# A planner's transfer price, its waits between engines and its table of shifts replaced

## The chip, the cores and the metric

The kernel runs on one core of a Trainium2 chip. The metric is the time of one execution on the device in microseconds (us). Engines are named as the profile names them: PE (TensorE), DVE (VectorE), ACT (ScalarE), POOL (GpSimd) and SP (SyncE, whose queue issues the transfers).

## The reference

Three stages follow one another. The output of one is the input of the next, and all inputs but q, k and v are weights.

```
# 1 attention: B=4, H=8, S=1152, D=64; queries averaged in pairs, so 576 rows
q_pool = q.reshape(B, H, S // 2, 2, D).mean(axis=3)
scores = (1 / np.sqrt(D)) * np.matmul(q_pool, k.transpose(0, 1, 3, 2))
scores = scores - np.max(scores, axis=-1, keepdims=True)
attn = np.exp(scores)
attn = attn / (np.sum(attn, axis=-1, keepdims=True) + 1e-09)
x = heads_side_by_side(np.matmul(attn, v))            # (4, 576, 512)
# 2 token mixing over the 576 rows, then a channel part
h = np.maximum(xt @ w_tok1, 0.0) @ w_tok2             # xt = x transposed; 576 -> 256 -> 576
u = x + h.transpose(0, 2, 1)
x = u + np.maximum(u @ w_ch1, 0.0) @ w_ch2            # 512 -> 1536 -> 512
# 3 Fourier mixing, a norm over the channels, a channel part
u = x + np.real(np.fft.fft(np.fft.fft(x, axis=1), axis=2))
un = (u - mean(u)) / np.sqrt(var(u) + 1e-06)
out = u + np.maximum(un @ w_ch1, 0.0) @ w_ch2         # 512 -> 2048 -> 512
```

The weights arrive as 64-bit floats.

## The kernel before, in words

Every fp32 operand of a product is split into a high and a low part of a shorter format, and a product is the sum of several matmuls of such parts. Attention works in 32 units, one for each batch and head: scores and their row maxima (line 655 on PE, line 662 on DVE, the exponential in line 665 on ACT), transposes of the exponentials (line 808), their split (line 812 on ACT, 815 on DVE) and the product with v (line 822). Some units at the start use another form (lines 758 to 773). Beside attention run the token mixing and the channel part of stage 2 for batches whose heads are done (lines 913 to 1051). Then come the Fourier mixing as matmuls with tables (line 1168), the norm and the transposes of line 1290, and the first channel rows of stage 3 (lines 1309 to 1347). The last stage is lines 1425 to 1514: products of line 1455 go into one of three PSUM banks, ACT copies them out (1465), DVE adds (1469), and line 1514 multiplies the result by the second weight.

A 64-bit weight is converted on the chip, in 62 pieces of up to 512 KB. Each piece has a buffer "slot" of a ring. SP loads it (line 375); ACT takes the absolute value of the high words (377) and turns the low words into floats (390); POOL clamps (379), DVE shifts, signs and masks (381, 384, 387), POOL multiplies and adds (392, 394), ACT takes the high part (397), POOL the low part (399), and SP stores the result to memory (410, 413), from where later steps load it again.

Nothing waits for a clock: each engine runs its own instructions in the order in which they are recorded, and stands still where the first of them waits, whatever is behind it. All transfers are issued by SP. The order is made before that by a planner, class Plan. Every step is added with a key, an engine, a cost in us, a due time, the steps that it depends on and the buffers that it takes or reads. SHIFT moves the due time of all steps of one key. The method "order" then replays the program: at each moment every free engine takes, of its ready steps, that with the earliest due time whose buffers are free. A step's end is the moment plus its cost; "lag" says how long after that a step on another engine may start, and "free_lag" when its buffers count as free. For a transfer, with t_dma as its cost, the replay reads

```
free["DMA"] = max(free.get("DMA", 0.0), now + 1.3) + best.cost
best.end, busy = free["DMA"] + 0.7, now + 0.35
```

so a transfer that finds no other ahead of it counts as landed 1.3 us, its cost and 0.7 us after its issue. The costs decide the order and nothing else.

## Time and profile before

| | us |
|---|---|
| median of three runs | 1481.97 |
| fastest, slowest run | 1467.82, 1483.97 |
| the profiled execution | 1484.98 |
| its span | 1482.9 |
| busy: PE, DVE, ACT, POOL | 1405.7, 981.3, 754.8, 573.9 |
| mean granted clock of TensorE | 0.976 of full speed |

The span is the time from the first to the last instruction that the profiler saw. In a timeline row the columns are start, duration, engine, line, operation, output and inputs, shapes and count; a bracket at the end tells how long the engine was idle before it and whose result ended that idle time. In a group row they are line, engine, operation, shapes and count, then busy time in all and the mean in ns, then idle time before the group and what ended it.

### The profile page before, as it was taken

How to read it: one execution, taken by the hardware profiler on the slowest of the kernel's cores; microseconds unless marked ns; L12 is line 12 of the kernel's file. 1: busy time of each engine (PE TensorE's matmuls, PEld its weight loads, DVE VectorE, ACT ScalarE, POOL GpSimd, SP SyncE). 2: the span in 40 equal slices, each digit the busy share in tenths (PEclk: the TensorE clock that was granted, in tenths of full speed). 3: DMA queues.
4: the chain of work that ended last, by engine and by line, in shares of the span. 5: the costliest groups of instructions: out<-in, count | busy, mean ns of one | idle time of the engine just before them, and what ended most of it. 6: DMA issues, size and time to landing. Idle time of an engine off the chain costs nothing.

```text
span 1482.9 us, 24363 instructions
## 1 busy us (share of the span) xinstructions
PE 1405.7 (95%) x9019; PEld 1281.9 (86%) x9019; DVE 981.3 (66%) x1830; ACT 754.8 (51%) x1534; POOL 573.9 (39%) x471
## 2 busy tenths in 40 slices
PE   7999989999999998998999999999899999999998
PEld 5777768899988898998999998999889888888887
DVE  6676547788876877887787776666555755465432
ACT  4444557866656766666785554422234443253230
POOL 4567766767668786685672001021010000000000
PEclk7999989999999999999999999999999999999999
DMA  7667658677758786776775216765074644544532
GB/s 176 181 191 194 175 182 247 211 209 245 229 148 270 182 258 203 219 216 201 235 207 161 86 57 180 262 199 163 17 232 151 217 160 157 181 159 153 174 110 93
DMA packets 112176, 270.34 MB, mean 182 GB/s; under 512 B 9971, under 2 KB 37748, under 8 KB 111767
## 3 DMA queue, kind: packets, MB, share of 16 engines
q1 hardware_dynamic: 112058, 268.79, 59.8%
q8 instruction: 71, 1.16, 0.3%
q14 instruction: 47, 0.39, 0.1%
HBM read 191.15 MB, written 44.86 MB: 159 GB/s over the span
## 4 chain that ended last, share of the span: by engine, by line
PE 63%; DMA 14%; DVE 7%; issue 6%; ACT 5%; POOL 3%; SPq 2%; ACTq 0%; DVEq 0%; POOLq 0%
PE bank L1455 8%; PE bank L1012 7%; PE y L1514 7%; PE bank L992 6%; PE m L655 5%; PE av L822 4%; PE av L769 4%; PE c L1514 4%; DMA slot<-in_wm_dram 4%; PE s L758 2%; PE bank L1325 2%; PE y L1347 2%; PE bank L689 2%; PE bank L808 2%; DVE nm L662 2%
## 5 line engine op out<-in xcount | busy, mean ns | idle before, releaser
L662 DVE TENSOR_REDUCE nm<-m 128x1 f32<-128x1152 f32 (+1 forms) x120 | 162.1, 1351 | 42.9 <-PE m L655 42.1
L992 PE MATMUL bank<-ut,w 128*128 128x320 f32 (+1 forms) x1152 | 178.4, 298 | 3.1 <-DVE yt L1021 2.0
L655 PE MATMUL m<-kk,qq 128*128 128x384 f32 (+1 forms) x720 | 157.8, 351 | 15.4 <-ACT s L665 15.2
L1455 PE MATMUL bank<-tt,wc 128*128 128x320 f32 x1008 | 161.5, 313 | 6.8 <-ACT e L1465 4.9
L665 ACT ACTIVATE s<-m,nm 128x1152 f32<-128x1152 f32 (+1 forms) x120 | 146.5, 1221 | 41.1 <-DVE nm L662 40.2
L1455 PEld LDWEIGHTS bank<-tt,wc 128*128 128x128 f32 x1008 | 149.4, 188 | 20.4 <-ACT e L1465 9.4
L1012 PE MATMUL bank<-h,w 128*128 128x320 f32 (+1 forms) x1152 | 164.3, 298 | 2.6 <-DVE yt L1021 1.3
L992 PEld LDWEIGHTS bank<-ut,w 128*128 128x128 f32 x1152 | 161.1, 190 | 4.4 <-DVE yt L1021 2.3
L1012 PEld LDWEIGHTS bank<-h,w 128*128 128x128 f32 x1152 | 156.6, 189 | 5.4 <-DVE pl L815 2.6
L655 PEld LDWEIGHTS m<-kk,qq 128*128 128x128 f32 (+1 forms) x720 | 119.8, 183 | 24.6 <-ACT s L665 19.7
L379 POOL TENSOR_SCALAR slot<-slot 128x512 f32<-128x512 f32 (+2 forms) x62 | 119.1, 1925 | 51.1 <-ACT slot L377 47.6
L822 PE MATMUL av<-ph,vv 128*128 128x256 f32 (+1 forms) x432 | 128.6, 317 | 0.5 <-DVE xtr L834 0.4
L812 ACT ACTIVATE ph<-bank 128x512 fp32r<-128x512 f32 (+1 forms) x192 | 90.1, 471 | 68.7 <-PE bank L808 67.0
L822 PE MATMUL av<-pl,vv 128*128 128x256 f32 (+1 forms) x432 | 119.7, 297 | 0.5 <-DVE pl L815 0.3
L815 DVE TENSOR_TENSOR pl<-bank,ph 128x512 fp32r<-128x512 f32 (+1 forms) x192 | 100.2, 523 | 23.2 <-ACT ph L812 22.2
L392 POOL TENSOR_TENSOR slot<-slot 128x512 f32<-128x512 f32 (+2 forms) x62 | 82.5, 1335 | 82.5 <-DVE slot L387 76.7
L1021 DVE TENSOR_TENSOR yt<-bank,yt 128x256 f32<-128x256 f32 (+1 forms) x192 | 85.7, 452 | 35.0 <-PE bank L1012 33.5
L1514 PE MATMUL y<-v,hp 128*128 128x512 f32 x432 | 104.8, 391 | 0.0
L1476 DVE SCALAR_TENSOR_TENSOR hp<-e,hp 128x320 fp32r<-128x320 f32 x96 | 41.7, 486 | 92.2 <-ACT hp L1474 91.9
L1474 ACT ACTIVATE hp<-e 128x320 fp32r<-128x320 f32 x96 | 38.3, 461 | 124.4 <-PE y L1514 116.8
L815 DVE TENSOR_TENSOR pl<-tr,ph 128x512 fp32r<-128x512 f32 (+1 forms) x144 | 79.2, 550 | 24.5 <-ACT ph L812 23.9
L808 PE MATMUL bank<-ident,s 128*128 128x128 f32 (+1 forms) x600 | 92.8, 270 | 0.7 <-DVE pl L815 0.6
(162 smaller groups left out, 2950.5 us busy)
## 6 DMA issues: line engine op xcount, KB each, us to landing
w<-wb_d SPq DMA_DIRECT2D x96, 512.0 KB
slot<-in_wm_dram SPq DMA_DIRECT2D x56, 512.0 KB
v<-w_d SPq DMA_DIRECT2D x24, 1024.0 KB
raw<-w_d SPq DMA_DIRECT2D x24, 896.0 KB
kk<-kx SPq DMA_DIRECT2D x66, 288.0 KB
wb_d<-slot SPq DMA_DIRECT2D x24, 512.0 KB
v<-in_v_dram SPq DMA_DIRECT2D x32, 292.5 KB
kx<-in_kT_dram SPq DMA_DIRECT2D x15, 576.0 KB
```

The costliest lines, as they stand in the source:

```text
L379: a = add("cclamp", "P", 0.155 + n * 0.00347, due, lambda: nc.gpsimd.tensor_scalar(out=f32(hi()), in0=f32(hi()), scalar1=F64_LO, scalar2=F ...
L655: nc.tensor.matmul(m.t[:n, :KW], qq.t[:r, t, q0:q0 + n], kk.t[:r, c * KW:(c + 1) * KW], start=(t == 0), stop=(t == 1))
L662: a = add("mx" + own_place, "V", t_dve(S), d + 0.05, lambda n=n, j=j: nc.vector.tensor_reduce(out=nm.t[:n, j:j + 1], in_=m_tile[0][:n, :, ...
L665: o = add("exp" + own_place, "A", t_act(S) + 0.18, d + 0.1, lambda s=s, n=n, j=j: nc.scalar.activation(out=s.t[:n].rearrange("p (c n) -> p ...
L808: nc.tensor.transpose(ps.t[:, at:at + r], made[j][0].t[:r, c * 128:(c + 1) * 128], ident[:r, :r])
L812: a = add("hi", "A", t_act(n), due + 0.1, lambda ps=ps, ph=ph, n=n: nc.scalar.activation(out=ph.t[:, :n], in_=ps.t[:, :n], func=AF.Copy), ...
L815: b = add("lo", "V", t_dve(n), due + 0.2, lambda ps=ps, ph=ph, pl=pl, n=n: nc.vector.tensor_tensor(out=pl.t[:, :n], in0=ps.t[:, :n], in1=f ...
L822: nc.tensor.matmul(po.t[:, :nq], vv.t[:, c].rearrange("p s d -> p (s d)"), x.t[:, k * nq:(k + 1) * nq], start=c == 0 and x is ph, stop=c = ...
L992: mms.append(lambda ps, k=len(mms), kk=kk, wi=wi, xi=xi, t0=t0, n=n: nc.tensor.matmul(ps[:, :n], view("p (s k n) -> p s k n", s=2, k=4)[:, ...
L1012: mms.append(lambda ps, k=len(mms), x=x, wi=wi, hi=hi, cc=cc, t0=t0, n=n: nc.tensor.matmul(ps[:, :n], ww[x][2]("p (s n) -> p s n", s=2)[:, ...
L1455: nc.tensor.matmul(ps.t[:, :PH], w.t[:, wi, k, 128 * kk:128 * kk + 128], x.t[:, xi, kk], start=(first and m == 0), stop=(last and m == 5), ...
L1514: nc.tensor.matmul(y.t, h.t[:, k, hi, j * 128:(j + 1) * 128], v.t[:, wi, k], start=(q == 0 and k == 0 and n == 0), stop=(q == 7 and k == 1 ...
```

## The change

The table SHIFT has new values for all its keys. A transfer costs its bytes over 235e3 instead of 390e3 per us, and the factors 1.2 and 1.75 on the loads and copies of q and k are gone. An engine is free only at the full end of a step, where the old account let the next step on ACT, DVE or POOL start 0.04 to 0.1 us earlier; every hop from one engine to another costs 0.2 us (0.26 to PE), a step on DVE that follows one on DVE 0.13 us, and buffers are free 0.2 us after a step's end. The lines of the changed kernel are those of the kernel before less 11. The computation, its steps and their tiles are the same.

```diff
@@ -60,26 +60,26 @@
 SHIFT = {
-    "cvld": -31.09, "cabs": 1541.59, "cclamp": 706.11, "cshift": 873.83, "csign": 145.68, "cexp": 661.87,
...
+    "cvld": -25.93, "cabs": 1270.21, "cclamp": 705.49, "cshift": 902.44, "csign": -44.94, "cexp": 832.42,
...
@@ -117,7 +117,7 @@
         self.key = key
         self.moves = eng in ("SP", "AQ")
         eng = "A" if eng == "AQ" else eng
-        self.eng, self.cost, self.due, self.emit, self.new, self.uses = eng, max(cost, 0.16) if eng == "V" else cost, due, emit, new, uses
+        self.eng, self.cost, self.due, self.emit, self.new, self.uses = eng, cost, due, emit, new, uses
         self.deps, self.after = deps, after
         self.end = None
         self.next = []
@@ -129,21 +129,10 @@
 SHARED = ("TL", "TA", "LL", "WL", "cshift", "csign", "cexp", "FPUT", "dwl", "yadd", "ql.", "kl.", "q.", "un")
 
 
-OVERLAP = {"A": 0.1, "V": 0.083, "P": 0.04}
-
-
 def lag(a, b):
-    if b == "T":
-        return 0.0 if a == "T" else 0.16 if a in OVERLAP else 0.26
-    if a == "T" or a not in OVERLAP or b not in OVERLAP:
-        return 0.2
-    if a == b == "A":
-        return -0.1
-    return 0.08 if b == "P" else 0.035
-
-
-def free_lag(a):
-    return 0.13 if a in OVERLAP else 0.2
+    if a == b:
+        return 0.13 if a == "V" else 0.0
+    return 0.26 if b == "T" else 0.2
 
 
 class Plan:
@@ -204,7 +193,7 @@
                     free["lock"] = best.end
                 elif eng == "P":
                     best.end += max(0.0, free.get("lock", 0.0) - now)
-                busy = best.end - OVERLAP.get(eng, 0.0)
+                busy = best.end
                 if best.moves:
                     free["DMA"] = max(free.get("DMA", 0.0), now + 1.3) + best.cost
                     best.end, busy = free["DMA"] + 0.7, now + 0.35
@@ -212,7 +201,7 @@
                         busy = max(busy, free["DMA"] - 1.5)
                 free[eng] = busy
                 heapq.heappush(wait, (busy, -1))
-                heapq.heappush(wait, (best.end + (0.2 if best.moves else free_lag(eng)), -1))
+                heapq.heappush(wait, (best.end + 0.2, -1))
                 out.append(best)
                 for o in best.next:
                     o.left -= 1
@@ -222,7 +211,7 @@
         return out
 
     def done(self, b, now):
-        return all(u.end is not None and u.end + (0.2 if u.moves else free_lag(u.eng)) <= now for u in b.users)
+        return all(u.end is not None and u.end + 0.2 <= now for u in b.users)
 
     def over(self, ring, now):
         for k, b in enumerate(ring.live if ring.any_slot else ring.live[:1]):
@@ -330,7 +319,7 @@
             return n * 0.00221 + 0.155
 
         def t_dma(n):
-            return n / 390e3
+            return n / 235e3
 
         def mm(*a, **k):
             return partial(nc.tensor.matmul, *a, **k)
@@ -598,9 +587,9 @@
             b, h = divmod(2 * p, H)
             kx, qx = Buf(kx_r), Buf(qx_r)
             due = 4 * p - 4.5
-            lq = add("lq", "SP", 1.2 * t_dma(128 * 8 * NQ), due, lambda: nc.sync.dma_start(
+            lq = add("lq", "SP", t_dma(128 * 8 * NQ), due, lambda: nc.sync.dma_start(
                 out=f32(qx.t), in_=qT[b, h:h + 2].rearrange("h d t n -> (h d) t n")), new=[qx])
-            lk = add("lk", "SP", 1.2 * t_dma(128 * 4 * S), due, lambda: nc.sync.dma_start(
+            lk = add("lk", "SP", t_dma(128 * 4 * S), due, lambda: nc.sync.dma_start(
                 out=f32(kx.t)[:, 1], in_=kT[b, h:h + 2].rearrange("h d n -> (h d) n")), new=[kx])
             q = add("qs", "P", t_pool(NQ), due + 0.5, lambda: nc.gpsimd.tensor_tensor(
                 out=f32(qx.t)[:, 1], in0=f32(qx.t)[:, 0], in1=f32(qx.t)[:, 1], op=ALU.add), [lq], uses=[qx])
@@ -618,18 +607,18 @@
                 kk, qq = Buf(kk_r), Buf(qq_r)
                 r = slice(64 * (g % 2), 64 * (g % 2) + 64)
                 d = 2 * g - 2.8
-                loads = [add("stk", "SP", 1.75 * t_dma(64 * 4 * S), d, lambda kk=kk, r=r: nc.sync.dma_start(
+                loads = [add("stk", "SP", t_dma(64 * 4 * S), d, lambda kk=kk, r=r: nc.sync.dma_start(
                     out=f32(kk.t)[:64], in_=f32(kx.t)[r, 0]), [kh], new=[kk], uses=[kx])]
-                loads.append(add("stq", "SP", 1.75 * t_dma(64 * 8 * NQ), d, lambda qq=qq, r=r: nc.sync.dma_start(
+                loads.append(add("stq", "SP", t_dma(64 * 8 * NQ), d, lambda qq=qq, r=r: nc.sync.dma_start(
                     out=f32(qq.t)[:64, :, :NQ], in_=f32(qx.t)[r]), [ql, qh], loads[:1], new=[qq], uses=[qx]))
-                loads.append(add("stk", "SP", 1.75 * t_dma(64 * 4 * S), d, lambda kk=kk, r=r: nc.sync.dma_start(
+                loads.append(add("stk", "SP", t_dma(64 * 4 * S), d, lambda kk=kk, r=r: nc.sync.dma_start(
                     out=f32(kk.t)[64:], in_=f32(kx.t)[r, 1]), [kl], loads[:1], uses=[kx, kk]))
-                loads.append(add("stq", "SP", 1.75 * t_dma(64 * 4 * NQ), d, lambda qq=qq, r=r: nc.sync.dma_start(
+                loads.append(add("stq", "SP", t_dma(64 * 4 * NQ), d, lambda qq=qq, r=r: nc.sync.dma_start(
                     out=f32(qq.t)[64:, 0, :NQ], in_=f32(qx.t)[r, 0]), [qh], loads[1:2], uses=[qx, qq]))
                 k2 = z = None
                 if g < ALONE:
                     k2 = Buf(k2_r)
-                    loads.append(add("stk", "SP", 1.75 * t_dma(64 * 4 * S), d, lambda k2=k2, r=r: nc.sync.dma_start(
+                    loads.append(add("stk", "SP", t_dma(64 * 4 * S), d, lambda k2=k2, r=r: nc.sync.dma_start(
                         out=f32(k2.t)[:64], in_=f32(kx.t)[r, 0]), [kh], loads[:1], new=[k2], uses=[kx]))
                 if g < ALONE + 3:
                     z = add("qz", "P", 0.4, 2 * g - 2.5, lambda qq=qq: nc.gpsimd.memset(f32(qq.t)[64:66, 1], 0.0), loads[1:2], uses=[qq])
```

On ACT, in the middle of attention: the place of the conversion step of line 390 (379 in the changed kernel) that stands at 557 us in the trace before, and the corresponding conversion in the new order. "slot" is the conversion's buffer, "s" the scores, "ph" a high part. Before:

```order
L812 ACTIVATE ph<-bank 128x320
L812 ACTIVATE ph<-tr 128x320
L812 ACTIVATE ph<-bank 128x320
L665 ACTIVATE s,sum_157<-m,nm 128x1152
L913 ACTIVATE h<-bank 128x256
L812 ACTIVATE ph<-tr 128x320
L812 ACTIVATE ph<-bank 128x320
L812 ACTIVATE ph<-tr 128x320
L390 ACTIVATE slot<-slot 128x512
L665 ACTIVATE s,sum_157<-m,nm 128x1152
L812 ACTIVATE ph<-bank 128x320
L377 ACTIVATE slot<-slot 128x512
```

and in the changed kernel:

```order
L801 ACTIVATE ph<-tr 128x512
L772 ACTIVATE vv<-v 128x9x64
L598 ACTIVATE qx<-qx 128x576
L654 ACTIVATE s,sum_157<-m,nm 128x1152
L858 ACTIVATE x_5744<-xs 128x5x64
L379 ACTIVATE slot<-slot 128x512
L366 ACTIVATE slot<-slot 128x512
L379 ACTIVATE slot<-slot 128x512
L801 ACTIVATE ph<-bank 128x256
L366 ACTIVATE slot<-slot 128x512
L654 ACTIVATE s,sum_157<-m,nm 66x1152
L902 ACTIVATE h<-bank 128x256
```

The exponential of line 665 stands right behind the conversion step before; in the new order three conversion steps stand together ahead of a split of line 801, and the last exponential of the unit comes three places after them.

On PE, in the last stage: runs of products of line 1455 (1444) among those of line 1514 (1503). Before:

```order
L1455 MATMUL bank<-tt,wc 128x320 x36
L1514 MATMUL y<-v_15294,hp 128x512 x3
L1455 MATMUL bank<-tt,wc 128x320 x6
L1514 MATMUL y<-v_15294,hp 128x512 x15
L1514 MATMUL c<-v_15397,hp 128x512 x9
L1455 MATMUL bank<-tt,wc 128x320 x36
L1514 MATMUL c<-v_15397,hp 128x512 x3
L1455 MATMUL bank<-tt,wc 128x320 x6
L1514 MATMUL y<-v_15397,hp 128x512 x18
L1514 MATMUL c<-v_15500,hp 128x512 x12
```

and in the changed kernel:

```order
L1503 MATMUL c<-v_15163,hp 128x512 x9
L1444 MATMUL bank<-tt,wc 128x320 x42
L1503 MATMUL c<-v_15163,hp 128x512 x3
L1503 MATMUL y<-v_15163,hp 128x512 x18
L1503 MATMUL c<-v_15282,hp 128x512 x9
L1444 MATMUL bank<-tt,wc 128x320 x42
L1503 MATMUL c<-v_15282,hp 128x512 x3
L1503 MATMUL y<-v_15282,hp 128x512 x18
L1503 MATMUL c<-v_15386,hp 128x512 x12
L1503 MATMUL y<-v_15386,hp 128x512 x18
```

Before, six products of the seven of a block stand together, three matmuls of another product follow, and then the seventh; now all seven stand together.

On ACT, the end of the conversions, where the steps of line 390 (379) are the last of the program. Before:

```order
L812 ACTIVATE ph<-bank 128x512
L812 ACTIVATE ph<-tr 128x512
L783 ACTIVATE vv<-v 128x9x64
L390 ACTIVATE slot<-slot 128x512
L377 ACTIVATE slot<-slot 128x512
L812 ACTIVATE ph<-bank 128x256
```

and in the changed kernel:

```order
L858 ACTIVATE x_8833<-xs 128x5x64
L379 ACTIVATE slot<-slot 128x512
L366 ACTIVATE slot<-slot 128x512
L1578 ACT_TABLE_LOAD
L1578 ACTIVATE rooted<-eps 128x1
L1588 ACTIVATE ny<-wraw 1x258
L902 ACTIVATE h<-bank 128x256
L1093 ACTIVATE cs<-wraw 97x870
L902 ACTIVATE h<-bank 128x320
L379 ACTIVATE slot<-slot 128x512
L386 ACTIVATE slot<-slot 128x512
L366 ACTIVATE slot<-slot 128x512
```

Before, the last conversion starts among the splits of attention and is the last for good; in the new order the last two stand among the first tables of the Fourier mixing (lines 1578 to 1588 and 1093).

## Rows read from the trace of the kernel before

**Rows 1.** The page, part 1: busy us, share, instructions by engine.

```profile
PE 1405.7 (95%) x9019; PEld 1281.9 (86%) x9019; DVE 981.3 (66%) x1830; ACT 754.8 (51%) x1534; POOL 573.9 (39%) x471
```

**Rows 2.** Stretches: us, busy PE, PEld, DVE, ACT, POOL, granted clock, DMA share, GB/s.

```profile
205.00:887.00 682.00, 650.34 (x4708) 622.28 (x4708) 532.78 (x933) 449.45 (x931) 412.64 (x325) 0.98 0.66 197
...
760.00:887.00 127.00, 126.20 (x950) 123.16 (x949) 93.25 (x166) 73.31 (x153) 25.77 (x20) 1.00 0.37 116
...
1105.00:1482.90 377.90, 366.37 (x1980) 322.17 (x1980) 193.04 (x333) 137.07 (x256) 0.00 (x0) 1.00 0.47 157
```

**Rows 3.** Timeline of PE: gaps of over 1.3 us, late ACT results.

```profile
27.65 0.61 PE L758 MATMUL s<-qq,kk 128*128 128x288 f32 x1 [1.83 <-ACT s L763]
67.01 0.82 PE L758 MATMUL s<-qq,kk 128*128 128x288 f32 x4 [2.19 <-ACT s L763]
104.67 0.92 PE L758 MATMUL s<-qq,kk 128*128 128x288 f32 x4 [3.10 <-ACT s L763]
133.93 1.36 PE L758 MATMUL s<-qq,kk 128*128 128x288 f32 x6 [1.31 <-ACT s L763]
196.71 0.54 PE L758 MATMUL s<-qq,kk 128*128 128x288 f32 x2 [2.85 <-ACT s L763]
478.73 0.66 PE L808 MATMUL tr<-ident,s 128*128 128x128 f32 x4 [1.69 <-DVE pl L815]
559.01 1.21 PE L655 MATMUL m<-kk,qq 128*128 128x384 f32 x3 [2.67 <-ACT s L665]
588.41 1.33 PE L655 MATMUL m<-kk,qq 128*128 128x384 f32 x6 [2.23 <-ACT s L665]
679.90 0.50 PE L808 MATMUL tr<-ident,s 128*128 128x128 f32 x3 [1.90 <-DVE pl L815]
701.96 1.60 PE L927 MATMUL bank<-x,w 128*128 128x512 f32 x4 [2.06 <-ACT yo L1051]
```

**Rows 4.** Timeline of ACT ahead of two of these gaps.

```profile
557.11 0.65 ACT L390 ACTIVATE slot<-slot 128x512 f32<-128x512 uint32 x1 [2.85 <-DMA slot<-in_wm_dram]
...
678.34 0.67 ACT L390 ACTIVATE slot<-slot 128x512 f32<-128x512 uint32 x1 [3.51 <-DMA slot<-in_wm_dram]
```

**Rows 5.** Groups by line, ACT, whole span.

```profile
L390 ACT ACTIVATE slot<-slot 128x512 f32<-128x512 uint32 (+2 forms) x62 | 41.3, 668 | 61.3 <-DMA slot<-in_wm_dram 33.3 <-DMA slot<-in_wt_dram 11.5 <-issue 7.3
```

**Rows 6.** Chain of waits that ended last: start, us, the 512 KB loads.

```profile
550.05 6.95 DMA slot<-in_wm_dram
...
672.60 5.63 DMA slot<-in_wm_dram
```

**Rows 7.** Stretches at the lower clock, columns as in rows 2.

```profile
67.70:71.10 3.40, 2.98 (x9) 1.96 (x9) 1.96 (x2) 2.47 (x7) 3.40 (x3) 0.51 0.77 180
...
702.50:705.90 3.40, 3.40 (x10) 2.69 (x9) 0.61 (x3) 1.83 (x4) 3.40 (x8) 0.50 0.99 192
...
432.90:439.70 6.80, 5.96 (x26) 5.92 (x27) 5.05 (x9) 3.44 (x7) 6.72 (x8) 0.50 0.33 99
...
1060.90:1067.70 6.80, 6.00 (x21) 6.00 (x22) 4.47 (x12) 1.89 (x5) 1.67 (x2) 0.50 0.00 0
```

**Rows 8.** Groups by line, PE, whole span.

```profile
L1455 PE MATMUL bank<-tt,wc 128*128 128x320 f32 x1008 | 161.5, 313 | 6.8 <-ACT e L1465 4.9 <-DVE e L1469 1.9
L655 PE MATMUL m<-kk,qq 128*128 128x384 f32 (+1 forms) x720 | 157.8, 351 | 15.4 <-ACT s L665 15.2
```

**Rows 9.** Timeline of PE in the last stage.

```profile
1218.36 2.91 PE L1455 MATMUL bank<-tt,wc 128*128 128x320 f32 x18
1221.61 2.90 PE L1455 MATMUL bank<-tt,wc 128*128 128x320 f32 x18 [0.34 <-ACT e L1465]
...
1440.24 6.41 PE L1455 MATMUL bank<-tt,wc 128*128 128x320 f32 x42
```

**Rows 10.** Timeline of PE at the first stretch of 6.8 us.

```profile
431.68 1.21 PE L992 MATMUL bank<-ut,w 128*128 128x256 f32 x8 [1.99 <-DVE yt L1021]
```

**Rows 11.** Timeline of PE where stage 3's channel part begins.

```profile
1059.56 0.66 PE L1290 MATMUL c<-ident,un 128*128 128x128 f32 x4 [3.04 <-DVE ut L1309]
```

More of the change, by code (lines that the diff above doesn't have):

```diff
@@ L62 @@
 SHIFT = {
-    "cvld": -31.09, "cabs": 1541.59, "cclamp": 706.11, "cshift": 873.83, "csign": 145.68, "cexp": 661.87,
-    "cword": 575.43, "cmul": -660.6, "cadd": 701.54, "chi": 55.64, "csub": -19.47, "cvst": -303.32, "cs":
-    -192.22, "warm.": -315.89, "l.": -1596.20, "q.": 202.71, "qh.": 1144.96, "ql.": 689.54, "kh.": -143.43,
-    "kl.": 2109.72, "M.": -1644.67, "mr.": 391.02, "zh.": -674.58, "mr2.": -1360.02, "zl.": -616.4, "mT.":
-    617.21, "mrow.": -1216.40, "vld": -220.98, "S.": -189.12, "exp.": 778.79, "AV.": -704.92, "xe.": 359.59,
[7 rows of a table removed]
@@ L75 @@
-    -25.81, "xa": -249.04, "open": -1612.80, "sqrt": -2293.90, "fcld": -1153.11, "fchi": 671.95, "fclo":
-    -556.82, "nyld": -1474.02, "nyh": 551.04, "fld": 78.08, "FPUT": 502.86, "DFT": 63.27, "Zh": 833.02, "Zl":
-    1207.75, "PB": -31.29, "PA": -31.1, "bs": -580.18, "pm": 170.7, "yadd": -451.44, "u2st": 466.64, "dwld":
-    -530.86, "dwv": 420.04, "dwh": -1294.44, "dwl": 1892.54, "mixover": -413.59, "fnetover": 474.16, "uld":
-    -523.87, "bn": 384.28, "bnr": 584.42, "un": 1404.47, "dturn": -337.23, "dth": -410.97, "dtl": -2174.20, "L":
@@ L80 @@
-    148.79, "drl": 344.24, "dll": 174.87, "dadd": 375.75, "dst": 99.64, "TB": 650.97, "TH": 1825.07, "TL":
-    -706.61, "TA": 584.16, "WR": 1074.40, "WH": 607.31, "WL": -528.71, "VR": -697.56, "LP": 147.59, "LE":
-    553.52, "LC": -973.26, "LH": 617.99, "LL": 377.03, "LQ": 1693.91,
+    "cvld": -25.93, "cabs": 1270.21, "cclamp": 705.49, "cshift": 902.44, "csign": -44.94, "cexp": 832.42,
+    "cword": 774.03, "cmul": -558.47, "cadd": 708.59, "chi": -53.24, "csub": -115.78, "cvst": -413.51, "cs":
@@ new lines @@
+    73.61, "warm.": -140.63, "l.": -1704.02, "q.": 351.07, "qh.": 1553.78, "ql.": 797.09, "kh.": -19.45, "kl.":
+    1892.97, "M.": -2130.55, "mr.": 433.1, "zh.": -685.21, "mr2.": -1605.04, "zl.": -866.61, "mT.": 452.86,
+    "mrow.": -843.49, "vld": -524.16, "S.": -408.9, "exp.": 741.3, "AV.": -1055.77, "xe.": -17.83, "turn":
[7 rows of a table added]
+    -425.22, "open": -1557.19, "sqrt": -2175.63, "fcld": -988.57, "fchi": 736.12, "fclo": -782.79, "nyld":
+    -1351.45, "nyh": 186.74, "fld": 108.37, "FPUT": 625.26, "DFT": 33.71, "Zh": 1221.35, "Zl": 1190.62, "PB":
@@ new lines @@
+    -31.25, "PA": -31.11, "bs": -454.93, "pm": 280.63, "yadd": -483.73, "u2st": 617.43, "dwld": -491.2, "dwv":
+    109.22, "dwh": -1442.53, "dwl": 2012.18, "mixover": -388.78, "fnetover": 785.38, "uld": -771.51, "bn":
+    183.78, "bnr": 707.04, "un": 1261.22, "dturn": -317.55, "dth": -715.08, "dtl": -2596.93, "L": 157.31, "drl":
+    185.99, "dll": 484.72, "dadd": 481.33, "dst": -84.03, "TB": 538.99, "TH": 2063.54, "TL": -508.2, "TA":
+    641.51, "WR": 855.14, "WH": 262.43, "WL": -497.16, "VR": -355.27, "LP": 206.65, "LE": 459.2, "LC": -1185.38,
@@ L83 @@
+    "LH": 628.53, "LL": 257.54, "LQ": 1903.14,
 }
```

14 rows, old and new, of the table SHIFT are left out of this document.

## The prediction

> **What bounds the kernel now.** The page's first part comes first: TensorE (PE) is busy for 1405.7 of 1482.9 us, 9,019 matmuls at a mean of 0.156 us (1405.7 / 9019), and no other engine passes 66% [rows 1]. Only 77.2 us are idle, so an order alone can take little. Next the table by stage, to see where that idle time lies: 31.7 us from 205 to 887 us (most of attention), 11.5 in the last stage, 34 in the rest; between 760 and 887 us, with few conversions left on POOL, PE misses 0.8 of 127 us [rows 2]. Then the timeline of PE, for who ends its gaps. Ten gaps of 1.3 to 3.1 us, 21.8 us in all, are ended by an ACT result (or by a DVE result that itself follows an ACT result) [rows 3]. The timeline of ACT at two of those places shows that ACT itself was not slow: it stood 2.85 and 3.51 us at the head of its queue before a line 390 instruction, the first step of a weight conversion, whose load had not landed, and the softmax copy or high-part copy that PE wanted was queued behind it [rows 4]. Over the run line 390 waits 33.3 + 11.5 us for its two kinds of load [rows 5], and the chain of waits holds these loads with 5.63 and 6.95 us each, 512 KB [rows 6]. So a late 512 KB load, a held ACT and a PE gap is the first thing that an order can mend.
>
> A gap costs twice. In the stretch just after seven of the ten gaps (after 67, 105, 134, 197, 559, 588 and 702 us) the granted clock is 0.50, the 1.2 GHz level, for 3.4 us; two of the seven rows stand here, the first and the last [rows 7]. PE stays busy in it at half speed, so each loses about 3.4 / 2 = 1.7 us.
>
> **The change, part by part.** Both orders hold the same instructions, the same 62 conversions and the same transfers; nothing is added or removed on any engine. What moves is the place of nearly every step in five queues, SP's (all transfers) included. I take the sum by stage against the profiled execution, 1484.98 us.
>
> 1. *Late loads that hold ACT.* Now: 21.8 us idle + 7 x 1.7 = 11.9 us of clock, together 33.7. The new price of a transfer is 390/235 = 1.66 times the old; for 512 KB the planner thus waits 4.2 us from issue instead of 3.3, still short of the 5.63 to 6.95 us that the rows show, so the correction is in the right direction but not whole. In the two orders I counted, for each of 248 loads, the matmuls that stand between the last one its issue waits behind and the first one that waits for its user: fewer than 40 for 6 loads before and 4 after, fewer than 45 for 11 and 7, fewer than 60 for 24 and 23. For the 56 conversion loads of this kind the median goes from 97 to 115, the shortest from 25 and 26 to 37 and 51. A load of 7 us needs 7 / 0.156 = 45 matmuls of cover. Thus the worst third to half of the short ones go; those between 45 and 60 are as many as before, and share queues with others. Bounds: nothing, and all 33.7. I take half, **-17**. The first order excerpt shows a conversion's first step moved.
> 2. *Last stage.* Line 1455 idles 6.8 us, ended by ACT's line 1465 and DVE's line 1469 [rows 8]; the timeline shows the pattern, a run of 18, a gap of 0.34, 18 more, where a run of 42 later has no gap [rows 9]. Runs of 36 with a wait in them go from 13 to 4, runs of 42 from 4 to 16 (second excerpt). Waits on a DVE sum with only one product of six matmuls in between go from 18 to 0, on an ACT copy from 31 to 24. Bounds 0 and -6.8; nearest is the run of 42 without a gap, so **-5**.
> 3. *Scores and maxima.* Line 655 idles 15.4 us, 15.2 ended by line 665 [rows 8]; 2.67 + 2.23 of it stand in step 1. The rest, 10.5 us over some 118 groups, hangs on how many matmuls stand between two groups: fewer than 17 in 4 places before and in 4 after. **0**; half of the rest, 5, either way.
> 4. *DVE behind POOL.* At 431 us PE idles 1.99 us behind DVE [rows 10], and the clock is at 0.50 for 6.8 us after it, 3.4 lost [rows 7]: 5.4. Conversions issued between matmul 1,000 and 4,000 fall from 36 to 29, so DVE and POOL are less crowded there, but one collision can return anywhere. Bounds 0 and -5.4, and no row is nearer to either; I take the middle, **-3**.
> 5. *Where FNet mixing meets the channel part,* 1059 us, PE waits 3.04 us for DVE [rows 11] and then loses 3.4 at the lower clock [rows 7]: 6.4. In the new order the twelve transposes of line 1290 that feed that DVE step still stand in one block on two banks. **0**; bounds -6.4 and, if a second such block goes uncovered, +3.0.
> 6. *Conversions moved back.* This pays for step 1. Eleven of the 62 conversions now begin behind matmul 4,563, where before the last began; the last begins at matmul 5,605 (third excerpt). Each brings its load and its stores on SP's queue, three passes on ACT, three on DVE and up to four on POOL into the stretch in which PE now misses 0.8 us of 127 [rows 2]. Their stores still land 1,281 matmuls ahead of the first load of the last stage that reads them (2,154 before), 200 us at 0.156, so nothing downstream is late. What they can cost is a held ACT, as at 557 us. POOL is busy 25.8 of 127 us there and the transfer engines 37% [rows 2], so their loads have a quieter time than those that hold ACT now. I take **0**; the upper bound is in the rivals.
>
> Sum: -17 - 5 + 0 - 3 + 0 + 0 = -25; 1484.98 - 25 = **1460 us**. The profiled time lies 3.0 above the median of the three runs, 1481.97, and those spread over 16 us, so I do not carry the 3.0 over.
>
> **A rule against the change.** The rows give 5.63 to 6.95 us for a 512 KB load on this crowded queue [rows 6]. By the Trainium skill, "DMA: Bandwidth & Descriptors", section "Anatomy of one DMA", a transfer takes about 2.0 us plus its bytes at 436 GB/s, by estimate 3.2 us for 512 KB, which is the old account's 3.3 and would leave nothing to gain in step 1; it is fitted on another path than this queue. By that rule the sum would be -8. The trace disagrees with its size, and the measurement decides.
>
> **Rivals.**
> - *No change: lateness is not a matter of the price.* If the loads that hold ACT are late because SP's queue is held by another transfer's wait, a longer price moves the whole queue and not the gap. For it: fewer than 60 matmuls of cover in 24 loads before and 23 after. Against: the shortest ones grew. Then step 1 is 0: 1485 - 8 = **1477 us**.
> - *All held loads are cured.* Steps 1, 2 and 4 at their full bounds: 33.7 + 6.8 + 5.4 = 45.9, **1439 us**. For it: the shortest conversion load now has 37 matmuls of cover, the next 51. Against: other loads under 45 remain.
> - *Slower: the conversions that moved back hold ACT.* Each of the eleven finds its load late in the dense stretch up to 887 us: a mean gap of 21.8 / 10 = 2.2 us plus 1.7 of clock, 3.9 each, 43 in all. Step 1 gives nothing but the conversions gone from earlier, 11/62 of some seven such gaps, -5; steps 2 and 4 give -8. 1485 + 43 - 13 = **1515 us**. For it: attention runs there too, and PE has no slack. Against: POOL and the transfers are quieter there. It passes +1% when (14.8 + 13) / 3.9, seven of the eleven, hold PE.
>
> **How the numbers follow.** About 1%, 14.8 us, is what a measurement of this kernel can tell from no change: faster is under 1467, slower over 1497. The forecast case (-10 to -36, that is 1449 to 1475) has 0.48, of which 0.09 lies above 1467; no change 0.26 (1472 to 1490); all cured 0.13 (1435 to 1446); slower 0.13. Faster: 0.39 + 0.13 = 0.52. Same: 0.09 + 0.26 = 0.35. Slower: 0.13. The range runs from 1440 to 1490: it leaves out the slower case and about half of the cured one, 0.2 in all.
>
> **What would show it.** In the changed kernel's profile: the idle time before the first conversion step (line 379 there) ended by its loads, now 44.8 us, at about half; PE gaps over 1.8 us before 760 us at four or five instead of ten, and as many fewer 3.4 us stretches at 0.50 (step 1); line 1444 idle under 3 us (step 2); line 644 idle about as now (step 3); PE missing under 2 us of the stretch before the last attention unit ends (step 6), where gaps with an ACT result behind a line 379 would show the slower rival; the junction's 3 us gap still there (step 5). I am wrong if the gaps' number stays and only their places change.

## The result and the profile after

The changed kernel takes 1428.09 us (median of four runs, 1426.96 to 1432.44) against 1482.64 before; the ratio is 0.9659 (95% interval 0.9595 to 0.9724). That is 54.5 us, 3.7%, less: below the range of 1440 to 1490, and more than twice the 25 us that the sum gave. The profiled execution took 1428.16 us, its span is 1426.2.

The first part of the page, and the chain of waits (part 4), after and then before:

```profile
PE 1379.3 (97%) x9019; PEld 1270.3 (89%) x9019; DVE 988.5 (69%) x1830; ACT 763.6 (54%) x1534; POOL 576.6 (40%) x471
...
PE 86%; DVE 6%; ACT 3%; issue 2%; DMA 1%; POOL 1%; SPq 0%; ACTq 0%; DVEq 0%; POOLq 0%
```

```profile
PE 63%; DMA 14%; DVE 7%; issue 6%; ACT 5%; POOL 3%; SPq 2%; ACTq 0%; DVEq 0%; POOLq 0%
```

PE does the same 9,019 matmuls in 26.4 us less busy time than in [rows 1], and is idle for 1426.2 - 1379.3 = 46.9 us instead of 77.2. Transfers, which held 14% of the chain before, hold 1%. The groups by line that answer to [rows 5] and [rows 8]:

```profile
L1444 PE MATMUL bank<-tt,wc 128*128 128x320 f32 x1008 | 157.7, 311 | 4.3 <-DVE e L1458 3.8 <-ACT e L1454 0.5
L644 PE MATMUL m<-kk,qq 128*128 128x384 f32 (+1 forms) x720 | 156.7, 349 | 4.6 <-ACT s L654 4.4
...
L747 PE MATMUL s<-qq,kk 128*128 128x288 f32 (+1 forms) x288 | 57.5, 323 | 0.5
...
L379 ACT ACTIVATE slot<-slot 128x512 f32<-128x512 uint32 (+2 forms) x62 | 41.0, 666 | 11.7 <-DMA slot<-in_wm_dram 11.4 <-DMA slot<-in_wt_dram 0.2
```

ACT's wait for conversion loads went from 44.8 us to 11.6, PE's idle time at line 655 (now 644) from 15.4 to 4.6. Line 747, before 758, the line of the five early gaps of [rows 3], idles 0.5 us. Four stretches at 1.2 GHz are left, 23.8 us together, where there were thirteen of 71.6 us. The two that are not in the first 32 us, columns as in [rows 2]:

```profile
185.00:191.80 6.80, 5.85 (x21) 5.54 (x22) 5.43 (x7) 5.66 (x11) 6.28 (x6) 0.50 0.31 122
...
717.50:724.30 6.80, 5.58 (x23) 5.57 (x23) 5.41 (x9) 1.12 (x3) 6.34 (x6) 0.50 0.20 80
```

So the gain is idle time, 30.3 us, and clock. The mean granted clock rose from 0.976 to 0.992: (1 - 0.976) x 1482.9 = 35.6 us lost before, (1 - 0.992) x 1426.2 = 11.4 now, 24.2 us gained. 30.3 + 24.2 = 54.5 of the 56.7 us of span.

The idle time went in the long gaps. In the timeline of PE nineteen gaps of over 1.3 us, 42.4 us in all, became six of 12.4; all other idle time together stayed, 34.8 and 34.5 us. The four of the six that lie behind the first 32 us:

```profile
185.95 1.33 PE L644 MATMUL m<-kk,qq 128*128 128x384 f32 x3 [2.56 <-ACT s L654]
397.27 0.36 PE L811 MATMUL av<-ph,vv 128*128 128x256 f32 x1 [1.94 <-DVE xtr L823]
486.89 0.47 PE L797 MATMUL bank<-ident,s 128*128 128x128 f32 x3 [1.75 <-DVE xs L855]
716.66 0.42 PE L811 MATMUL av<-ph,vv 128*128 128x320 f32 x1 [1.63 <-DVE xtr L823]
```

### The profile page after: what moved, and what is told of

It is laid out like the page before. It is cut to its first block, busy times and chain, and to the rows that moved or that the text cites. A ratio compares the mean times of both kernels' runs of the same rounds, so it can differ in the third digit from the quotient of the medians.

```text
span 1426.2 us, 24338 instructions
## 1 busy us (share of the span) xinstructions
PE 1379.3 (97%) x9019; PEld 1270.3 (89%) x9019; DVE 988.5 (69%) x1830; ACT 763.6 (54%) x1534; POOL 576.6 (40%) x471
## 4 chain that ended last, share of the span: by engine, by line
PE 86%; DVE 6%; ACT 3%; issue 2%; DMA 1%; POOL 1%; SPq 0%; ACTq 0%; DVEq 0%; POOLq 0%
PE bank L981 10%; PE bank L1001 10%; PE bank L1444 10%; PE m L644 9%; PE av L811 7%; PE y L1503 7%; PE c L1503 5%; PE av L758 4%; PE bank L797 4%; PE tr L797 3%; PE bank L678 3%; PE s L747 2%; PE bank L1314 2%; PE y L1336 2%; PE bank L916 2%; PE c L1157 2%
## 5 line engine op out<-in xcount | busy, mean ns | idle before, releaser
L1444 PE MATMUL bank<-tt,wc 128*128 128x320 f32 x1008 | 157.7, 311 | 4.3 <-DVE e L1458 3.8
L654 ACT ACTIVATE s<-m,nm 128x1152 f32<-128x1152 f32 (+1 forms) x120 | 146.2, 1218 | 18.4 <-DVE nm L651 17.9
L801 ACT ACTIVATE ph<-bank 128x512 fp32r<-128x512 f32 (+1 forms) x192 | 89.6, 470 | 71.5 <-PE bank L797 69.8
L381 POOL TENSOR_TENSOR slot<-slot 128x512 f32<-128x512 f32 (+2 forms) x62 | 80.7, 1302 | 102.4 <-DVE slot L376 98.6
L1458 DVE TENSOR_TENSOR e<-bank,e 128x320 f32<-128x320 f32 x96 | 47.1, 491 | 106.4 <-PE bank L1444 70.7
L1454 ACT ACTIVATE e<-bank 128x320 f32<-128x320 f32 x72 | 31.3, 434 | 129.4 <-PE bank L1444 129.4
L801 ACT ACTIVATE ph<-tr 128x512 fp32r<-128x512 f32 (+1 forms) x144 | 70.4, 489 | 54.5 <-PE tr L797 44.9
```

What stands on the lines that cost most here:

```text
L654: o = add("exp" + own_place, "A", t_act(S) + 0.18, d + 0.1, lambda s=s, n=n, j=j: nc.scalar.activation(out=s.t[:n].rearrange("p (c n) -> p ...
L801: a = add("hi", "A", t_act(n), due + 0.1, lambda ps=ps, ph=ph, n=n: nc.scalar.activation(out=ph.t[:, :n], in_=ps.t[:, :n], func=AF.Copy), ...
L1444: nc.tensor.matmul(ps.t[:, :PH], w.t[:, wi, k, 128 * kk:128 * kk + 128], x.t[:, xi, kk], start=(first and m == 0), stop=(last and m == 5), ...
```

## The experiments

In the table below, for all of them: "idle" is the span less PE's busy time, "clock" is 1 less the mean granted clock, times the span, and "ACT" is ACT's idle time that transfers ended, summed over the view of its waits. All three are of the profiled execution, which in e3 is 12 us and in e10 7 us under the median; the time is the median, the ratio is to the runs of the kernel before on the same chip. The experiments ran on five chips, on which the kernel before stands at 1480.1 to 1483.7 us in the median.

| kernel | price, hops, table | us | ratio (95%) | idle | clock | ACT |
|---|---|---|---|---|---|---|
| before | old, old, old | 1482 | | 77.2 | 35.6 | 90.4 |
| changed | new, new, new | 1428.1 | 0.966 (0.960-0.972) | 46.9 | 11.4 | 32.1 |
| e1 late use | before, ACT moved | 1471.3 | 0.992 (0.989-0.995) | 70.5 | 28.0 | 53.9 |
| e2 load half | changed, loads moved | 1458.2 | 0.984 (0.981-0.987) | 64.8 | 23.3 | 76.7 |
| e3 | old, new, new | 1510.2 | 1.020 (1.015-1.026) | 87.7 | 40.4 | 106.9 |
| e4 | new, 0.205, new | 1467.5 | 0.990 (0.986-0.993) | 67.7 | 27.8 | 31.3 |
| e5 | old, 0.205, old | 1499.1 | 1.013 (1.007-1.019) | 90.7 | 30.0 | 93.1 |
| e6 | 230e3, new, new | 1451.7 | 0.980 (0.975-0.986) | 61.8 | 15.9 | 26.8 |
| e7 | new, new, old | 1460.7 | 0.986 (0.981-0.991) | 65.2 | 24.8 | 29.5 |
| e8 | new, old, new | 1469.7 | 0.992 (0.990-0.995) | 74.1 | 25.0 | 22.0 |
| e9 | new, old, old | 1458.5 | 0.983 (0.978-0.988) | 61.8 | 26.2 | 21.2 |
| e10 | old, new, old | 1523.8 | 1.026 (1.020-1.033) | 101.5 | 50.0 | 121.7 |
| e11 | old, old, new | 1514.2 | 1.020 (1.015-1.026) | 97.2 | 42.4 | 81.7 |
| e12 | 385e3, old, old | 1502.4 | 1.011 (1.005-1.018) | 89.6 | 40.6 | 77.2 |
| e13 | new for conversion loads | 1475.2 | 0.996 (0.994-0.999) | 73.7 | 26.5 | 58.1 |
| e14 | new for all others | 1457.6 | 0.985 (0.982-0.988) | 63.5 | 24.7 | 28.8 |
| e15 | changed, ACT moved | 1450.0 | 0.981 (0.978-0.983) | 56.6 | 17.4 | 21.3 |
| e16 | e10, ACT moved | 1499.1 | 1.014 (1.010-1.018) | 86.1 | 44.9 | 65.1 |
| e17 | before, ACT and DVE moved | 1493.0 | 1.007 (1.004-1.010) | 87.4 | 22.4 | 45.5 |
| e18 | changed, DVE moved | 1475.9 | 0.996 (0.994-0.999) | 80.4 | 22.1 | 23.9 |

In every row, the span less idle and clock leaves 1363 to 1381 us (before 1370.1, changed 1367.9): between the two kernels the order changes little else. The widest are e10, 7 us under before, and e17, 11 us over it; why, no view shows.

**e1, e16 and e15: the held ACT taken away.** In three orders, the two first conversion steps on ACT are recorded later; the other queues stay.

```diff
+        # cword (line 390) and cabs (line 377): recorded right ahead of the POOL step that needs them
-        for o in self.order():
+        for o in self.late(self.order(), ("cword", "cabs")):
```

e1, on the kernel before:

> The kernel before with its order kept on PE, DVE, POOL and SP; only ACT's two first steps of each conversion (lines 377 and 390) are recorded right ahead of the POOL step that needs them, so that ACT does other work while the load is on its way. Conversion loads with fewer than 45 matmuls of cover fall from 5 to 1. Theory A (late loads hold ACT, PE starves behind it, and the clock falls after each gap): idle time before line 390 ended by its loads from 44.8 us to under 20, PE gaps over 0.9 us from 27 to about 15, time 1435 to 1460 us. Theory B (the gain is the careful account of the short waits between engines, everywhere in the order): the order of the other engines is the old one, so 1470 to 1490 us.

ACT's wait for its loads fell to 16.9 us, as theory A said, but not the time: 1471.3 lies in theory B's range, at its lower end. 10 us were gained, clear of noise, where 28 us of wait went. e16, on e10's order, where ACT waited longest:

> The kernel of e10 (new hops, old table and price, 1524 us, ACT's wait for conversion loads 74 us) with ACT's two first conversion steps recorded right ahead of the POOL step that needs them; all other queues as in e10. If the held ACT is the channel, its wait falls to about 35 us and the time by 25 to 40: 1484 to 1499. If the price acts through the other queues' order: 1510 to 1524.

The medians differ by 24.7 us, the two profiled spans by 19.3, and the ratios, each against the kernel before on its own chip, by some 18: a gain at or below the lower end of what the held ACT was to give. ACT's wait fell further than expected, to 19 us, and part of it came back elsewhere: DVE's first conversion step waits 23.5 us for POOL where it waited 9.9. ACT's waits for conversion loads in e10, and then in e16 (waits by engine: total, times, longest):

```profile
ACT slot L379 <- DMA slot<-in_wm_dram: 63.0, 27, 7.3
...
ACT slot L379 <- DMA slot<-in_wt_dram: 10.8, 3, 9.5
```

```profile
ACT slot L379 <- DMA slot<-in_wm_dram: 18.0, 7, 7.5
...
ACT slot L379 <- DMA slot<-in_wt_dram: 1.0, 2, 0.8
```

e15, on the changed kernel:

> The changed kernel with ACT's two first conversion steps recorded right ahead of the POOL step that needs them, as in e1; all other queues as in the changed kernel. ACT's wait for conversion loads, 11.6 us, under 5. If a held ACT still costs about as much as it waits: 1418 to 1426. If the pick has already placed those waits where PE has cover: 1426 to 1432. If moving ACT's order breaks what the pick had: 1432 to 1445.

It lost 22 us, more than any of its ranges had, although the first conversion step on ACT now waits only 3.3 us. DVE's first conversion step shows what took its place, in the changed kernel and in e15:

```profile
L370 DVE TENSOR_SCALAR slot<-slot 128x512 int32<-128x512 int32 (+2 forms) x62 | 44.1, 715 | 14.7 <-POOL slot L368 8.6 <-DMA kk<-kx 6.0
```

```profile
L383 DVE TENSOR_SCALAR slot<-slot 128x512 int32<-128x512 int32 (+2 forms) x62 | 46.8, 758 | 32.4 <-POOL slot L381 32.3
```

POOL's clamp follows ACT's step. Move ACT's and the clamp is late, and DVE, whose queue is unchanged, stands behind it, 32.3 us instead of 8.6. The same wait is 28.8 us in the kernel before, and 36.8 in e1:

```profile
L381 DVE TENSOR_SCALAR slot<-slot 128x512 int32<-128x512 int32 (+2 forms) x62 | 48.2, 786 | 29.0 <-POOL slot L379 28.8
```

**e2: the loads made late again.** In the changed kernel each conversion load is recorded half way to its first user.

```diff
+        # cvld goes to the place (its own + that of its first user) // 2
-        for o in self.order():
+        for o in self.later(self.order()):
```

> The changed kernel with each conversion load recorded half way between its own place and that of its first user; all else as in the changed kernel. Conversion loads with fewer than 45 matmuls of cover rise from 3 to 9, under 60 from 8 to 18. Theory A: six to ten more held ACTs at about 3.9 us each, 1450 to 1470 us, with the wait before line 379 for its loads back above 35 us. Theory B: the other queues' order is the new one, 1425 to 1440 us.

1458.2, 30 us lost, as theory A said; ACT's wait for these loads is 53.7 + 3.5 us:

```profile
L395 ACT ACTIVATE slot<-slot 128x512 f32<-128x512 uint32 (+2 forms) x62 | 40.9, 664 | 62.4 <-DMA slot<-in_wm_dram 53.7 <-issue 5.2 <-DMA slot<-in_wt_dram 3.5
```

That any move in this order costs time, as e15 and e4 below also show, could explain the loss as well. The trace of e2 speaks for the held ACT: PE's idle time grew by 17.9 us, and seven gaps of 1.3 to 3.9 us, 15.0 us together, stand right behind an ACT wait of 1.8 to 4.5 us for a conversion load. The changed kernel has none of over 0.5 us that does. The longest, on ACT, DVE and PE:

```profile
642.93 0.67 ACT L395 ACTIVATE slot<-slot 128x512 f32<-128x512 uint32 x1 [3.85 <-DMA slot<-in_wm_dram]
645.14 0.49 DVE L921 SCALAR_TENSOR_TENSOR h<-bank,h 128x320 fp32r<-128x320 f32 x1 [3.26 <-ACT h L918]
645.69 0.58 PE L997 MATMUL bank<-ut,w 128*128 128x256 f32 x1 [3.87 <-DVE h L921]
```

**e3 and e7 to e11: each of the three parts alone and in pairs.** With the two kernels they are all eight combinations. The edits are the change's own lines, taken or undone; some of them stand here for each part:

```diff
 # e3 (undone), e9 (alone): the price, with the factors 1.2 and 1.75
-            return n / 390e3
+            return n / 235e3
 # e8 (undone), e10 (alone): lag, free_lag, OVERLAP, the least cost on DVE
-    return 0.08 if b == "P" else 0.035
+    return 0.26 if b == "T" else 0.2
 # e7 (undone), e11 (alone): SHIFT
```

> The changed kernel planned with the old transfer price (390e3, with the factors 1.2 and 1.75); table and waits between engines are the new ones. Theory A, read by cover: conversion loads under 45 matmuls 4 (3 in the changed kernel), under 80 23 (15): 1430 to 1450 us. Theory P (the price alone made the gain): back to 1465 to 1485. Theory S (any order other than the one chosen with this table is worse): 1445 to 1475, and e4 too.

> The changed kernel's account (price, hops, no overlap) with the table of the kernel before. Theory S: neither is the table of this account nor this order picked, so it is a neighbour without a pick: the account alone is worth what this stands below e5; by S with a careful account 1455 to 1480, with ACT's wait for conversion loads under 20 us by the longer price. Theory T (the account makes nothing, the table all): 1480 to 1520.

> The changed kernel planned with the old hops, overlaps and free times between engines; table and transfer price are the new ones. ACT's wait for conversion loads stays under 20 us (the price is the new one). Theory A (cover decides): 1428 to 1440. Theory S: 1455 to 1480. Theory B (the careful hops make the gain): 1475 to 1500, above e4 and e6.

> The kernel before planned with the new transfer price (235e3, without the factors); table, hops and overlaps are the old ones. Theory P+S (an order that nobody picked stands near 1500 us with the old price and near 1460 with the new one; a pick takes 20 to 30 us more): 1450 to 1480, ACT's wait before line 390 for its loads under 20 us. If the price is not the part that counts: 1490 to 1515.

> The kernel before planned with the new hops, without overlaps; table and transfer price are the old ones. Theory P+S: the price is the old one, so 1490 to 1515, ACT's wait for conversion loads above 35 us. If the hops count as much as the price: 1450 to 1480.

> The kernel before planned with the new table; price, hops and overlaps are the old ones. Theory P+S: 1490 to 1525, ACT's wait for conversion loads above 35 us. If the table itself carries the gain: 1430 to 1470.

e3 was slower than any theory had it, and e10, at 1523.8, 9 us above its range; the other four fell where the price puts them. Read the table by the price: with the old one 1510, 1524 and 1514 us, with the new one 1461, 1470 and 1458. In the four pairs that differ in the price alone the new price is faster every time, by 24 (before, e9), 63 (e10, e7), 45 (e11, e8) and 82 us (e3, changed). The hops and the table have no such sign: from old to new the hops alone make 42 us more to 42 less, the table alone 32 more to 33 less, by what they are planned with. e3's line 379, with the changed kernel's table and hops, and then e9's line 390, with the old ones:

```profile
L379 ACT ACTIVATE slot<-slot 128x512 f32<-128x512 uint32 (+2 forms) x62 | 40.9, 666 | 69.9 <-DMA slot<-in_wm_dram 48.3 <-DMA slot<-in_wt_dram 7.8 <-issue 7.6
```

```profile
L390 ACT ACTIVATE slot<-slot 128x512 f32<-128x512 uint32 (+2 forms) x62 | 41.4, 670 | 8.6 <-DMA slot<-in_wm_dram 8.5
```

**e4, e5, e6 and e12: neighbours of the two kernels.** One cost is changed by a few per cent.

```diff
 # e4 (changed kernel)
-    return 0.26 if b == "T" else 0.2
+    return 0.26 if b == "T" else 0.205
 # e5 (before)
-        return 0.2
+        return 0.205
 # e6 (changed kernel)
-            return n / 235e3
+            return n / 230e3
 # e12 (before)
-            return n / 390e3
+            return n / 385e3
```

> The changed kernel planned with 0.205 instead of 0.2 us for a hop between engines, nothing else; the order differs in most places all the same. Theory A, read by cover: conversion loads under 45 matmuls 6 instead of 3, of all loads 12 instead of 5: 1438 to 1455 us. Theory B: the account is as careful as before, 1425 to 1438. Theory S: 1445 to 1475.

> The kernel before planned with 0.205 instead of 0.2 us for a hop from PE or a transfer, nothing else; as in e4 the order differs in most places. Theory S (each table belongs to one order that was picked among many; any neighbour of it is some 2 to 3% worse, whichever account): 1505 to 1530 us, as far above the kernel before as e4, 1467.5, stands above the changed kernel, 1428. Theory C (the changed kernel is lucky, the kernel before is an ordinary order of its account): 1470 to 1495.

> The changed kernel planned with 230e3 instead of 235e3 bytes per us, nothing else. Conversion loads have as much cover as in the changed kernel (3 under 45 matmuls, median 111). Theory S: 1455 to 1475, like e4, with the wait of ACT for loads as small as in the changed kernel and the lost time in gaps of every other kind. Theory A (cover decides): 1425 to 1435.

> The kernel before planned with 385e3 instead of 390e3 bytes per us, nothing else: a second neighbour of the kernel before, the counterpart of e6. Theory P+S: 1490 to 1520, like e5. If e5 was a chance and the kernel before is an ordinary order of its account: 1470 to 1490.

All four are slower than the kernel that they neighbour, e4 by 39, e5 by 18, e6 by 24 and e12 by 19 us. e4 and e12 lie in the range of theory S; e5, at 1499.1, and e6, at 1451.7, fell some us below theirs, above those of the rivals. The loads do not explain e4: its line 379 waits less than the changed kernel's. What it has more of is gaps elsewhere, on PE behind ACT's line 654 and DVE's line 804 (waits by engine):

```profile
L379 ACT ACTIVATE slot<-slot 128x512 f32<-128x512 uint32 (+2 forms) x62 | 40.9, 665 | 6.2 <-DMA slot<-in_wm_dram 3.8 <-POOL slot L368 1.6 <-issue 0.8
```

```profile
PE m L644 <- ACT s L654: 12.8, 9, 3.1
PE tr L797 <- DVE pl L804: 4.9, 6, 1.6
PE bank L797 <- DVE pl L804: 4.5, 5, 1.6
```

**e13 and e14: by which transfers the price acts.**

```diff
 # e13, on the kernel before
-            o = add("cvld", "SP", t_dma(1024 * n), due, lambda: nc.sync.dma_start(
+            o = add("cvld", "SP", 390 / 235 * t_dma(1024 * n), due, lambda: nc.sync.dma_start(
 # e14: 235e3 for all, and 235 / 390 * t_dma(1024 * n) here
```

> The kernel before planned with the new transfer price for the 62 conversion loads alone; all other transfers, the table and the hops as before. If the conversion loads carry the price's worth (step 1): 1455 to 1475, like e9, with ACT's wait for them under 15 us. If the rest carries it: 1490 to 1510.

> The counterpart of e13: the new price for every transfer but the conversion loads. If the conversion loads carry the price's worth: 1485 to 1515, ACT's wait for conversion loads above 35 us. If the rest carries it: 1455 to 1475.

e14 fell where the rest carries the worth: 1457.6, as fast as e9 with the new price for all. e13 fell between: 1475.2 is the top of its first range and 15 us under the second, and ACT's wait for these loads, 21.2 us, is not under 15. Against e5 and e12, at 1499 to 1502, the conversion loads alone are worth some 25 us and the rest alone some 43, so the two overlap. The replay has one queue of transfers ("DMA" in its table of free times), so a longer price for the others also puts the conversion loads later in the plan. That is how I read it, and no run tests it by itself; line 390 waits 7.6 us for its loads of this kind in e14, instead of 33.3.

**e17 and e18: DVE's conversion steps moved too.** The steps of lines 381, 384 and 387 are recorded right ahead of POOL's product, in e17 together with ACT's.

```diff
-        for o in self.order():
+        for o in self.late(self.order(), ("cword", "cabs", "cshift", "csign", "cexp")):  # e18: the last three
```

> The kernel before with ACT's two first conversion steps and DVE's three (lines 377, 390, 381, 384, 387) each recorded right ahead of the step that needs its result; PE, POOL and SP as before. If a conversion costs by holding ACT and DVE: ACT's wait for its loads under 20 us, DVE's wait for POOL at line 381 under 12, time 1440 to 1455 (e1 with ACT's steps alone: 1471). If conversions no longer matter once ACT is free: 1465 to 1475. If POOL, which now waits in their place, holds q and k up: 1475 to 1495.

> The changed kernel with DVE's three conversion steps (lines 370, 373, 376) recorded right ahead of the POOL step that needs them; all else as in the changed kernel. DVE waits 8.6 us for POOL at line 370 now. If that wait still costs what it lasts: 1418 to 1426. If the pick has placed it beside cover: 1426 to 1434. If any move breaks the pick, as in e15: 1438 to 1452.

e17, at 1493.0, is 12 us slower than before and lies in its third range, e18, at 1475.9, is 48 us slower than the changed kernel and above all of its ranges. In both DVE waits less for POOL, and PE is idle for longer. In e17 PE does not wait for q or k, as the third range supposed, but for DVE's split, 14.8 us where the kernel before has 4.4:

```profile
PE tr L828 <- DVE pl L835: 14.8, 15, 2.4
```

Its idle time is 10 us more than before and its clock loss 13 us less, so that its loss of time lies in PE's busy time, unexplained. In the timeline of e18's DVE, and then of its PE, at one such place:

```profile
670.85 1.04 DVE L390 TENSOR_SCALAR slot<-slot 128x512 int32<-128x512 int32 x1
671.93 0.69 DVE L393 SCALAR_TENSOR_TENSOR slot<-slot 128x512 int32<-128x512 int32 x1
672.65 0.43 DVE L396 TENSOR_SCALAR slot<-slot 128x512 int32<-128x512 int32 x1
673.00 0.48 DVE L824 TENSOR_TENSOR pl<-bank,ph 128x320 fp32r<-128x320 f32 x1
```

```profile
673.53 0.77 PE L1001 MATMUL bank<-ut,w 128*128 128x256 f32 x4 [2.37 <-DVE pl L824]
```

The three steps, busy and waiting for nothing, stand ahead of the split that PE needs, and PE waits 2.37 us. An engine that works at the wrong moment costs PE as much as one that waits.

## Why the prediction was wrong

**The way was right, the size was not.** Of 54.5 us the sum had 25.

- *Step 1, late loads that hold ACT: -17, "I take half".* This is the term that failed most, by its size. All ten gaps are gone, and with them the seven stretches at 1.2 GHz behind them: not half but the whole 33.7 us. Of the six gaps of over 1.3 us that are left only that at 185.95 stands at a line of the ten, and it has its like before at 209.28, which was not among them. Ten were also too few. Beside them and those of steps 4 and 5, seven more gaps of over 1.3 us stood in the trace before, 15.5 us; three of these, behind the first 32 us, were ended by ACT as well, and two of them are part of what step 3 put at nothing. One of those two, and the third:

```profile
209.28 1.01 PE L655 MATMUL m<-kk,qq 128*128 128x384 f32 x2 [2.86 <-ACT s L665]
922.74 0.64 PE L1046 MATMUL bank<-ident,yt 128*96 128x128 f32 x4 [2.80 <-ACT yo L1051]
```

Lines 655, 758 and 808 (tr) idled 31.6 us before, and at 644, 747 and 797 (tr) it is 5.6; waits, mostly on DVE, took some of this back, 15.0 us more at lines 678, 797 (bank), 811, 843 and 981 together than at their counterparts before. Two of the three rows of before, of which [rows 8] has the third:

```profile
L808 PE MATMUL tr<-ident,s 128*128 128x128 f32 (+1 forms) x480 | 73.2, 267 | 4.5 <-DVE pl L815 4.4
L758 PE MATMUL s<-qq,kk 128*128 128x288 f32 (+1 forms) x288 | 61.3, 337 | 11.7 <-ACT s L763 11.5
```

The held ACT as a cause is shown by the gaps of e2, where the loads are late again, and by e16, which takes 55 us of ACT's wait for these loads away and gains 18 to 25. The wait is not paid in full: e1 gave 10 us for 28. Nor was it all conversion loads: in the timeline of ACT seven of the ten gaps stand behind a wait for one, that at 588 us behind a load of k, that at 702 behind a store, that at 105 behind POOL. My two ways of halving the term were poor. The count of matmuls between a load's issue and its user told little: the changed kernel has 3 conversion loads under 45 matmuls, e4 has 6 and waits less for them. And a price that falls short of 5.63 us was taken for half a cure, while every order as it was planned with 230e3 or 235e3 for all transfers, whatever its table, has ACT wait 21 to 32 us for transfers, and every one with 385e3 or 390e3 for all, 77 to 122.
- *Clock outside the sum.* The sum priced 18.7 of the 35.6 us that the lower clock cost. Of the rest, the 20.5 us at 1.2 GHz in the first 34 us became 10.2, and two more stretches of 3.4 us went; one of 6.8, at 717.5, is new.
- *Step 2, last stage: -5.* Measured 6.8 to 4.3, -2.5. The waits on ACT went but for one, but before the last product of 17 of the 24 runs of 42 there is now a short one on DVE; my count had such waits fall to 0. One run:

```profile
1348.72 5.44 PE L1444 MATMUL bank<-tt,wc 128*128 128x320 f32 x36
1354.38 1.14 PE L1444 MATMUL bank<-tt,wc 128*128 128x320 f32 x6 [0.23 <-DVE e L1458]
```

- *Step 3, scores and maxima: 0.* Measured -10.8 at that line, of which 4.9 are step 1's two gaps. I had ascribed the other gaps to the spacing of the matmuls, which is the same in both orders; most of them went all the same, so spacing was not what made these.
- *Step 4, DVE behind POOL: -3.* I priced one place. Its gap of 1.99 us and its stretch at the lower clock are gone, -5.4, though line 992, now 981, idles 5.0 us in all instead of 3.1. DVE's idle time at line 381 behind POOL was 28.8 us over the run and is 8.6 at line 370. A view by group would have shown it.
- *Step 5, the junction: 0, "still stand in one block".* It went: one wait of 3.04 us became three of 0.33 to 0.62, and the 6.8 us at the lower clock behind it are gone. The twelve transposes are still one block on PE; why DVE was earlier, no run tells.

```profile
1006.69 0.66 PE L1279 MATMUL c<-ident,un 128*128 128x128 f32 x4 [0.33 <-DVE zn L1164]
1007.77 0.65 PE L1279 MATMUL c<-ident,un 128*128 128x128 f32 x4 [0.42 <-DVE ut L1298]
1009.04 2.69 PE L1157 MATMUL c<-ss,fold 96*128 96x290 f32 x18 [0.62 <-DVE ut L1298]
```

- *Step 6, conversions moved back: 0.* Right: with POOL busy 67.5 of 130 us there, PE misses 1.05 us.

```profile
725.00:855.00 130.00, 128.95 (x978) 126.33 (x977) 105.05 (x194) 83.32 (x174) 67.53 (x62) 1.00 0.53 165
```

**The rivals.** "All held loads are cured" (0.13) gave 1439 and was nearest; even it left out the junction and line 655. "No change" gave 1477 and fell with the result, "slower" with step 6. By the Trainium skill, "DMA: Bandwidth & Descriptors", section "Anatomy of one DMA", a transfer takes about 2.0 us plus its bytes at 436 GB/s, by estimate 3.2 us for 512 KB. The traces do not agree for this queue: the 512 KB conversion loads of the changed kernel took 6.0 us in the median from issue to landing. The rival that followed from that rule, nothing to be had from the price, fell with the four pairs above.

**What made the 54 us.** The five orders with the old price and without the table made for their costs (e3, e5, e10, e11, e12) stand at 1499 to 1524, mean 1509.9; the five with the new one (e4, e6, e7, e8, e9) at 1452 to 1470, mean 1461.6. The price is worth 48 us between these means. The two kernels are each better than their neighbours, 1481.4 (the median of before beside e1 to e4) by 28.5 and 1428.1 by 33.5. So of the gain some 48 us are the transfer price and some 5 the better choice of an order, if the five of each kind stand for all orders of their price; they differ among themselves by 25 and 18 us, so that 5 cannot be told from nothing. Hops and overlaps show no worth of their own: they make the order faster or slower by what they are planned with. That a table fits only its exact costs is shown by e4, e5, e6 and e12; that these tables were found by search is how I read it, and no run shows it. Open is by which waits the last 30 us of such a choice go: e15, e17 and e18 moved one or two queues and each made another wait.

## What to carry to other kernels

When an order is planned, first put the cost of a transfer nearer to what the trace shows, crowded queue and all: here the longer price was faster in all four pairs. Even so it counts 4.2 us for 512 KB; a price that meets the measured 6.0 was not run. Price a planned order by all its long gaps and the clock lost behind them, on whichever engine they wait: here the gaps of over 1.3 us were the whole gain in idle time, and I had priced twelve of nineteen. And expect a tuned order to lose 1 to 3% when any cost of its planner is touched: compare accounts between several orders each, never between one and one.
